# One copy and two stores at the end of a decode block, and a bias load in eight pieces

## The chip, the cores and the metric

The kernel runs on one core of one Trainium2 chip. The core has five engines that run side by side: TensorE for matrix products, VectorE, ScalarE and GpSimd for elementwise work, and SyncE, which issues DMAs and waits. DMAs are issued from SyncE's and from ScalarE's queue and carried out by 16 DMA engines. The metric is the device time of one execution in microseconds (us), as the median of several runs; the span of a profile is a little shorter than that time (188.2 us in a run that took 190.38).

## The reference

One decode step for a batch of two rows of 448 numbers. The normalised row goes into two branches, and both are added to the input. Branch A is attention over the last 4096 positions of a cache (16 query heads, 8 key heads of 256), branch B a dense pair with the Mish activation and a bias `b1`.

```python
x = A_x                                   # [2, 1, 448]
xn = layernorm(x)
q = (xn @ A_wq)                           # 16 heads of 256
p = softmax(q k^T / 16)                   # the last 4096 positions of the cache
A = (p v) @ A_wo                          # [2, 1, 448]
h = xn @ B_w1 + B_b1                      # [2, 1, 1792]
B = (h * tanh(softplus(h))) @ B_w2        # [2, 1, 448]
out = x + A + B
```

## The kernel before

The sum `x + A + B` is held in PSUM by TensorE. It is not kept as 2 rows of 448, but as four groups of 112 columns: group g stands on the partitions 32g and 32g+1 (one per batch row), so that four products can stand side by side in the array. The shape of the sum and its seed, and the way everything is added to it:

```python
x_bf = consts.tile([Bsz, D], BF16)                       # Bsz = 2, D = 448
nc.scalar.dma_start(out=x_bf[:, :], in_=A_x.flatten_outer_dims())      # L125
b1_sb = consts.tile([P, 2, NI], BF16)                    # P = 128, NI = 7
nc.scalar.dma_start(out=b1_sb[:], in_=B_b1.rearrange("(k q c) -> q k c", k=2, q=P))  # L127
load_k(0, 0)                                             # SyncE: keys, wq, keys, w1 ...
...
id2 = consts.tile([Bsz, Bsz], FP32)
nc.vector.tensor_copy(out=id2[:], in_=ident[0:Bsz, 0:Bsz])
...
nc.scalar.activation(out=rstd[:], in_=mv[:, 1:2], func=ACT.Sqrt, ...)  # L160, layernorm
nc.vector.reciprocal(out=rstd[:], in_=rstd[:])
... # VectorE: xn, masks, rows of xn; TensorE turns them; VectorE writes xs (L220)
early = ps_e.tile([Bsz, D], FP32)       # x and the first heads of A are summed here
acc = ps_a.tile([P, DG], FP32)          # DG = 112: the sum in four groups

def carry():                            # early -> acc, which starts the four groups
    e_sb = small.tile([P, 2 * Dh], FP32, tag="vs", name="e_sb", bufs=1)[0:Bsz, 0:D]
    nc.scalar.copy(out=e_sb, in_=early[:])
    for g in range(G):                  # G = 4
        nc.tensor.matmul(
            acc[32 * g : 32 * g + Bsz, :],
            lhsT=id2[:],
            rhs=e_sb[:, g * DG : (g + 1) * DG],
            start=True, stop=False, skip_group_check=True,
        )

def add_rows(lhsT, rows, stop=False):   # L249: the last heads of A, and all of B
    for g in range(G):
        nc.tensor.matmul(acc[32 * g : 32 * g + Bsz, :], lhsT=lhsT,
                         rhs=rows[:, g * DG : (g + 1) * DG], start=False, stop=stop, ...)
...
# VectorE turns each load of keys (L269); mish() reads b1_sb (L518)
```

The end of the program, behind the last part of the dense output:

```python
finish(u)
mix(u)
for part in range(len(w2_parts)):
    dense_out(part)                     # 56 products of L249, in parts as w2 lands

res = consts.tile([Bsz, D], BF16)
for g in range(G):
    dst = res[:, g * DG : (g + 1) * DG]
    src = acc[32 * g : 32 * g + Bsz, :]
    if g % 2 == 0:
        nc.vector.tensor_copy(out=dst, in_=src)          # L620
    else:
        nc.scalar.copy(out=dst, in_=src)                 # L622
nc.sync.dma_start(out=out.flatten_outer_dims(), in_=res[:])   # L623
```

Of the kernel before, what the change touches and what calls it, by code (L numbers as in the profile page):

```python
# [11 lines left out]
BF16 = mybir.dt.bfloat16  # L12
FP32 = mybir.dt.float32
# [4 lines left out]
def kernel(  # L18
# [13 lines left out]
    nc = tc.nc  # L32
    P = 128
    G = 4
# [4 lines left out]
    Bsz, Sq, D = A_x.shape  # L39
# [21 lines left out]
    DG = D // G  # L61
# [13 lines left out]
    consts = ctx.enter_context(tc.tile_pool(name="consts", bufs=1))  # L75
# [48 lines left out]
    x_bf = consts.tile([Bsz, D], BF16)  # L124
    nc.scalar.dma_start(out=x_bf[:, :], in_=A_x.flatten_outer_dims())  # L125
    b1_sb = consts.tile([P, 2, NI], BF16)
    nc.scalar.dma_start(out=b1_sb[:], in_=B_b1.rearrange("(k q c) -> q k c", k=2, q=P))  # L127

    load_k(0, 0)
    wq_t = []  # L130
# [7 lines left out]
    ident = consts.tile([P, P], BF16)  # L138
# [2 lines left out]
    nc.gpsimd.memset(qd[:], 0.0)  # L141
    ones = consts.tile([P, P], BF16)
    nc.gpsimd.memset(ones[:], 1.0)
    id2 = consts.tile([Bsz, Bsz], FP32)
    nc.vector.tensor_copy(out=id2[:], in_=ident[0:Bsz, 0:Bsz])
    hot = consts.tile([P, KU, 4, 32, KU], BF16)
    nc.gpsimd.memset(hot[:], 0.0)
    for k in range(KU):
        nc.gpsimd.tensor_copy(
            out=hot[:, k, :, :, k], in_=ident[:].rearrange("p (q y) -> p y q", y=4)  # L150
# [10 lines left out]
        out=rstd[:], in_=mv[:, 1:2], func=ACT.Sqrt, bias=eps_t[:], scale=1.0  # L161
# [4 lines left out]
        out=xn_bf[:],  # L166
# [8 lines left out]
        out=parm[:], in_=ident[:].rearrange("p (a o) -> p o a", o=2), axis=AXIS.X, op=ALU.add  # L175
# [3 lines left out]
        out=jm[:],  # L179
        in_=ident[:].rearrange("p (a j h) -> p j a h", j=J, h=rep),  # L180
# [4 lines left out]
        out=jm[:], in0=jm[:], scalar1=-1.0, scalar2=29952.0, op0=ALU.add, op1=ALU.mult  # L185
# [3 lines left out]
        out=mneg[:], in_=jm[:].unsqueeze(1).to_broadcast([P, TH * 8, J])  # L189
    )  # L190
    sel = consts.tile([P, 2, NQ], FP32)
    for x in range(2):
        for w in range(4):
            at = 32 * w + (2 * (w % 2) + x) * NQ
            src = ident[:, at : at + NQ]
            if w == 0:
                nc.vector.tensor_copy(out=sel[:, x, :], in_=src)
            else:
                nc.vector.tensor_tensor(
                    out=sel[:, x, :], in0=sel[:, x, :], in1=src, op=ALU.add  # L200
# [16 lines left out]
    for odd in range(2):  # L217
        for half in range(2):
            o = (half + odd) % 2
            nc.vector.tensor_scalar(  # L220
                out=xs[:, odd::2, half * Bsz : (half + 1) * Bsz],
# [10 lines left out]
    acc = ps_a.tile([P, DG], FP32)  # L232

    def carry():
        e_sb = small.tile([P, 2 * Dh], FP32, tag="vs", name="e_sb", bufs=1)[0:Bsz, 0:D]
        nc.scalar.copy(out=e_sb, in_=early[:])
        for g in range(G):
            nc.tensor.matmul(
                acc[32 * g : 32 * g + Bsz, :],
                lhsT=id2[:],  # L240
                rhs=e_sb[:, g * DG : (g + 1) * DG],
                start=True,
                stop=False,
                skip_group_check=True,
            )
# [31 lines left out]
    for n in range(2):  # L277
        for e in range(2):
# [3 lines left out]
                out=sp[:],  # L282
                in_=ident[:, o : o + 63 : 2].unsqueeze(1).to_broadcast([P, G, 32]),
# [316 lines left out]
    for g in range(G - 1):  # L600
        values(u, g)
        if g == 0:
            relay(u - 1)
            mix_early(u - 1)
            carry()
# [6 lines left out]
    for part in range(len(w2_parts)):  # L612
        dense_out(part)

    res = consts.tile([Bsz, D], BF16)
    for g in range(G):
        dst = res[:, g * DG : (g + 1) * DG]
        src = acc[32 * g : 32 * g + Bsz, :]
        if g % 2 == 0:
            nc.vector.tensor_copy(out=dst, in_=src)  # L620
        else:
            nc.scalar.copy(out=dst, in_=src)  # L622
    nc.sync.dma_start(out=out.flatten_outer_dims(), in_=res[:])  # L623


# [28 lines left out]
```

The softmax here doesn't subtract the row's maximum and nothing guards it: scores larger than these inputs give would overflow.

## Time and profile before

| what | value |
|---|---|
| time, median of 3 runs | 190.56 us (190.56 to 190.72) |
| span of the profile | 188.2 us |
| TensorE busy | 92.1 us (49%) |
| VectorE busy | 89.1 us (47%) |
| ScalarE busy | 12.3 us (7%) |
| moved by DMA | 77.78 MB, 413 GB/s on average |

The profile gives each engine's busy time, the span in 40 slices with a digit for the busy tenths of each, the DMA queues, the chain of waits that ended last (followed back from the last instruction), and the groups of instructions, each with its tile, its shape and what ended the idle time before it. In the lines, PE is TensorE's matmul, PEld its loading of weights, DVE VectorE, ACT ScalarE, SPq and ACTq the queues on which SyncE and ScalarE issue DMAs; q1 is SyncE's DMA queue, q10 ScalarE's. L620 is line 620 of the kernel. Names of tiles are without their numbers, so that `b_sb` is `b1_sb`, and `w<-in_B_w_dram` is a load of `w1` or `w2`.

### The profile page before, as it was taken

The page shows a single profiled execution, that of the slowest core. Times are in us where ns is not written, and L with a number is a line of the kernel's source. Part 1 is how long each engine was busy: PE and PEld are TensorE (multiplying, and loading weights), DVE is VectorE, ACT ScalarE, POOL GpSimd, SP SyncE. Part 2 cuts the span into 40 slices and gives each one's busy share as a digit, 9 for nine tenths or more (in the row PEclk, how much of TensorE's full clock was granted, in tenths as well). Part 3 has the DMA queues.
Part 4 walks back from the last instruction along what each step waited for, and adds up shares of the span by engine and source line. Part 5 has one row for each costly group of instructions (what it writes and reads, how often), then busy time and mean ns, then how long its engine had stood idle before and what let it go on. Part 6 is the DMA issues. An engine that isn't in the chain of part 4 may idle for free.

```text
span 188.2 us, 1989 instructions
## 1 busy us (share of the span) xinstructions
PE 92.1 (49%) x873; PEld 37.6 (20%) x873; DVE 89.1 (47%) x81; ACT 12.3 (7%) x23; POOL 4.0 (2%) x16
## 2 busy tenths in 40 slices
PE   0301545564139003888647033868464044968473
PEld 0100121521013001423112011413121011513261
DVE  6619643984980098008940395029910692040001
ACT  3000031001000100110001000110001001011101
POOL 8000000000000000000000000000000000000000
PEclk9999999558555855555556655555558555559965
DMA  6999999999999999999999999999998999999990
GB/s 223 446 390 409 440 432 428 470 442 390 428 449 418 428 426 411 466 446 400 435 463 411 414 435 434 429 442 414 463 460 383 418 431 432 435 398 452 411 391 31
DMA packets 5871, 77.78 MB, mean 413 GB/s; under 512 B 868, under 2 KB 1640, under 8 KB 2408
## 3 DMA queue, kind: packets, MB, share of 16 engines
q1 hardware_dynamic: 5588, 77.66, 96.8%
q8 instruction: 6, 0.10, 0.2%
q10 hardware_dynamic: 276, 0.01, 0.1%
q14 instruction: 1, 0.01, 0.0%
HBM read 77.67 MB, written 0.00 MB: 413 GB/s over the span
## 4 chain that ended last, share of the span: by engine, by line
DMA 80%; PE 10%; DVE 3%; issue 3%; SPq 2%; ACT 1%; DVEq 0%
DMA v<-in_A_v_cache_dram 59%; DMA k<-in_A_k_cache_dram 15%; DMA w<-in_B_w_dram 6%; PE pv L392 5%; DVE kt L269 2%; PE sc L347 2%; PE o L412 1%; PE acc L249 1%; PE dn L370 1%; SPq L134 1%; SPq L97 1%; DVE p L358 0%; SPq L105 0%; ACT ex L355 0%; ACT vs L406 0%
## 5 line engine op out<-in xcount | busy, mean ns | idle before, releaser
L269 DVE STREAM_TRANSPOSE kt<-k 128x4096 f32<-128x4096 f32 x16 | 70.0, 4414 | 39.9 <-DMA k<-in_A_k_cache_dram 39.9
L392 PE MATMUL pv<-v,p 128*32 128x512 bf16 x240 | 26.8, 593 | 54.1 <-DMA v<-in_A_v_cache_dram 54.1
L347 PE MATMUL sc<-kt,qd 128*32 128x512 bf16 x256 | 27.3, 599 | 3.2 <-DVE kt L269 1.9
L392 PEld LDWEIGHTS <-p 128*32 128x32 bf16 x240 | 8.4, 124 | 70.8 <-issue 65.2
L439 DVE TENSOR_TENSOR oT<-o,rec 128x16 bf16<-128x16 f32 x4 | 0.7, 174 | 28.8 <-PE o L412 16.3
L358 DVE STREAM_TRANSPOSE p<-ex 128x512 bf16<-128x512 bf16 x8 | 5.2, 690 | 16.0 <-ACT ex L355 16.0
L347 PEld LDWEIGHTS <-qd 128*32 128x32 bf16 x256 | 8.6, 134 | 19.8 <-issue 17.9
L355 ACT ACTIVATE ex<-sc 128x512 bf16<-128x512 f32 x8 | 4.8, 597 | 74.1 <-PE sc L347 74.1
L291 PE MATMUL q_ps<-wq,xs 128*32 128x512 bf16 x28 | 3.4, 624 | 11.8 <-DMA wq<-in_A_wq_dram 11.8
L474 PE MATMUL early<-wo,ox 128*2 128x448 bf16 x24 | 8.0, 500 | 0.8 <-ACT ox L464 0.8
L412 PE MATMUL o<-sel,vs 128*128 128x8 f32 x32 | 6.7, 339 | 2.8 <-ACT vs L406 2.8
L412 PEld LDWEIGHTS o<-sel,vs 128*128 128x128 f32 x32 | 6.4, 293 | 6.0 <-ACT vs L406 6.0
L370 PE MATMUL dn<-p,ones 128*128 128x512 bf16 x8 | 4.3, 541 | 6.0 <-DVE p L358 6.0
L406 ACT COPY vs<-pv 128x512 f32<-128x512 f32 x4 | 2.3, 586 | 49.4 <-PE pv L392 49.4
L504 PE MATMUL h_ps<-xs,w 128*128 128x4 bf16 x49 | 2.8, 193 | 4.6 <-DMA w<-in_B_w_dram 4.6
L336 PE MATMUL sc<-mneg,ident 128*128 128x512 bf16 x8 | 4.8, 594 | 0.0
L212 PE MATMUL xr_ps<-ident,xrows 2*128 2x2 bf16 x7 | 1.0, 181 | 6.6 <-DVE xrows L211 6.6
L378 DVE TENSOR_REDUCE rec<-dn 128x8 f32<-128x512 f32 x4 | 2.8, 692 | 2.5 <-PE dn L370 2.5
L291 PEld LDWEIGHTS <-xs 128*32 128x32 bf16 x28 | 1.0, 126 | 13.8 <-issue 13.8
L504 PEld LDWEIGHTS <-w 128*128 128x128 bf16 x49 | 2.7, 157 | 5.2 <-DMA w<-in_B_w_dram 5.2
L474 PEld LDWEIGHTS <-ox 128*2 128x2 bf16 x24 | 2.3, 105 | 4.6 <-issue 3.0
L455 PEld LDWEIGHTS <-hot 128*64 128x64 bf16 x48 | 2.0, 141 | 2.8 <-issue 2.8
(62 smaller groups left out, 37.7 us busy)
## 6 DMA issues: line engine op xcount, KB each, us to landing
k<-in_A_k_cache_dram SPq DMA_DIRECT2D x8, 4096.0 KB, 30.0
v<-in_A_v_cache_dram SPq DMA_DIRECT2D x15, 2048.0 KB, 27.0
wo<-in_A_wo_dram SPq DMA_DIRECT2D x3, 896.0 KB, 23.7
wq<-in_A_wq_dram SPq DMA_DIRECT2D x1, 2048.0 KB, 16.7
w<-in_B_w_dram SPq DMA_DIRECT2D x1, 1568.0 KB, 31.9
wq<-in_A_wq_dram SPq DMA_DIRECT2D x1, 1536.0 KB, 19.7
v<-in_A_v_cache_dram SPq DMA_DIRECT2D x1, 1536.0 KB, 9.7
wo<-in_A_wo_dram SPq DMA_DIRECT2D x2, 448.0 KB, 15.4
```

What stands on the lines that cost most here:

```text
L269: nc.vector.transpose(out=kt[i][:, :, :, r, :], in_=t[:, r * KE : (r + 1) * KE].bitcast(FP32).rearrange("p (a c j) -> p a c j", c=P // (R ...
L291: nc.tensor.matmul(q_ps[32 * u : 32 * (u + 1), :], lhsT=xs[:, s, :], rhs=wq_t[s][:, u * 512 : (u + 1) * 512], start=(s == 0), stop=(s == N ...
L336: nc.tensor.matmul(sc[:].rearrange("p t c m -> p (t c m)"), lhsT=ident[:], rhs=mneg[:].rearrange("p a j -> p (a j)"), start=True, stop=Fal ...
L347: nc.tensor.matmul(sc[32 * w : 32 * (w + 1)].rearrange("p t c m -> p t (c m)"), lhsT=qd[:, u, 2 * n + e, :, :].rearrange("p g q -> p (g q) ...
L355: nc.scalar.activation(out=ex[:, :, :, i, :], in_=sc[:], func=ACT.Exp, scale=scale)
L358: nc.vector.transpose(out=p_t[h][:].rearrange("p g t q -> p t g q"), in_=ex[:, h * TH : (h + 1) * TH].rearrange("p t c i m -> p t (c i m)" ...
L370: nc.tensor.matmul(dn[:].rearrange("p a q -> p (a q)"), lhsT=ones[:], rhs=p_t[i][:].rearrange("p g t q -> p (g t q)"), start=(i == 0), sto ...
L378: nc.vector.tensor_reduce(out=rec[:], in_=dn[:].rearrange("p a q -> p q a"), axis=AXIS.X, op=ALU.add)
L392: nc.tensor.matmul(pv[32 * w : 32 * (w + 1), :, :].rearrange("p x d -> p (x d)"), lhsT=p_t[a // 4][:, g, 4 * (a % 4) : 4 * (a % 4) + 4, :] ...
L412: nc.tensor.matmul(po[:, c, :], lhsT=sb[:, x, c::2], rhs=sel[:, x, :], start=(x == 0 and c == 0), stop=(last and x == 1), skip_group_check ...
L474: nc.tensor.matmul(early[:], lhsT=ox[:, i, :], rhs=w[:, i, :], start=False, stop=(u == U - 2 and i == 7),)
L504: nc.tensor.matmul(h_ps[:, i, :, :].rearrange("p k b -> p (k b)"), lhsT=w1_v[:, s, i, :], rhs=xs[:, s, 0 : 2 * Bsz], start=(s == 0), stop= ...
```

## The change

The last step is rearranged. The sum stands on the partitions 0, 1, 32, 33, 64, 65, 96 and 97. In place of four copies of two partitions, two on VectorE and two on ScalarE, one VectorE copy takes all 98 partitions from 0 to 97. The copied tile then holds the row of batch b in four runs of 112 numbers, on the partitions b, 32+b, 64+b and 96+b. Two stores bring them to their places in the output: ScalarE issues that of batch row 0, SyncE that of batch row 1.

So that the partitions in between hold something defined, the seed of the sum is widened: the identity is 2x32 in place of 2x2 (the other 30 columns are zero), and the seeding product writes all 32 partitions of each group. Apart from that, the diff cuts the load of the bias into eight loads of 16 partitions each, all on ScalarE's queue.

```diff
     b1_sb = consts.tile([P, 2, NI], BF16)
-    nc.scalar.dma_start(out=b1_sb[:], in_=B_b1.rearrange("(k q c) -> q k c", k=2, q=P))
+    b1_in = B_b1.rearrange("(k q c) -> q k c", k=2, q=P)
+    for lo in range(0, P, 16):
+        nc.scalar.dma_start(out=b1_sb[lo : lo + 16], in_=b1_in[lo : lo + 16])
@@
-    id2 = consts.tile([Bsz, Bsz], FP32)
-    nc.vector.tensor_copy(out=id2[:], in_=ident[0:Bsz, 0:Bsz])
+    id2 = consts.tile([Bsz, 32], FP32)
+    nc.vector.tensor_copy(out=id2[:], in_=ident[0:Bsz, 0:32])
@@ carry()
-                acc[32 * g : 32 * g + Bsz, :],
+                acc[32 * g : 32 * (g + 1), :],
                 lhsT=id2[:],
@@ the end
-    res = consts.tile([Bsz, D], BF16)
-    for g in range(G):
-        dst = res[:, g * DG : (g + 1) * DG]
-        src = acc[32 * g : 32 * g + Bsz, :]
-        if g % 2 == 0:
-            nc.vector.tensor_copy(out=dst, in_=src)
-        else:
-            nc.scalar.copy(out=dst, in_=src)
-    nc.sync.dma_start(out=out.flatten_outer_dims(), in_=res[:])
+    last = 32 * (G - 1) + Bsz
+    res = consts.tile([P, DG], BF16)
+    nc.vector.tensor_copy(out=res[0:last, :], in_=acc[0:last, :])
+    rows = out.rearrange("b s (g e) -> b (s g) e", g=G)
+    for b, queue in ((0, nc.scalar), (1, nc.sync)):
+        queue.dma_start(out=rows[b], in_=res[b : last - 1 + b : 32, :])
```

## The prediction

> **What bounds the kernel now.** I read the page's slices first, because they tell whether one resource is full from end to end. Each digit is the busy share of a slice of 4.7 us, in tenths:
>
> ```profile
> DMA  6999999999999999999999999999998999999990
> GB/s 223 446 390 409 440 432 428 470 442 390 428 449 418 428 426 411 466 446 400 435 463 411 414 435 434 429 442 414 463 460 383 418 431 432 435 398 452 411 391 31
> q1 hardware_dynamic: 5588, 77.66, 96.8%
> q10 hardware_dynamic: 276, 0.01, 0.1%
> ```
>
> The 16 DMA engines are busy in all but the first and the last slice, and 96.8% of what they can do is spent on SyncE's queue (q1), which carries 77.66 MB. So the kernel is a stream of loads with a short head and a short tail. ScalarE's queue (q10) costs 0.1%. The chain of waits says the same from the other side: 80% of the span is DMA, and from 2.52 us on the chain goes from one load to the next. Then I read its last pieces (start, length, what):
>
> ```profile
> 172.06 12.12 DMA w<-in_B_w_dram
> 184.17 0.04 issue
> 184.22 0.78 PE acc L249 x17
> 184.99 0.20 issue
> 185.19 0.45 PE acc L249 x11
> 185.64 0.24 DVE res L620
> 185.89 0.30 DVEq L649
> ```
>
> The last load lands at 184.17 us and the span ends at 188.2, so 4.0 us stand behind the stream. They belong to 28 matmuls (to 185.64), the copies of the sum, the store and the end of the program. The timeline gives the copies and the store, and the waits of SyncE give the landing of the store:
>
> ```profile
> 185.62 0.56 DVE L620 CAST res<-acc 2x112 bf16<-2x112 f32 x2 [3.63 <-PE acc L249]
> 185.66 0.52 ACT L622 CAST res<-acc 2x112 bf16<-2x112 f32 x2 [7.60 <-PE acc L249]
> 186.25 0.33 SPq L623 DMA_DIRECT2D out_dram<-res  x1
> SPq L649 <- DMA out_dram<-res: 0.6, 1, 0.6
> ```
>
> Two copies run one behind the other on each engine, so both are done at 186.18 us, and the store is issued 0.07 us later. The issue ends at 186.58, SyncE then waits 0.6 us for the data to land, about 187.2, and the last 1.0 us is the closing of the program. Last, the diff splits the bias load, so I looked at the head of the timeline:
>
> ```profile
> 0.73 0.53 ACTq L125 DMA_DIRECT2D x_bf<-in_A_x_dram  x1
> 1.29 0.42 ACTq L127 DMA_DIRECT2D b_sb<-in_B_b_dram  x1
> 1.75 1.28 ACT L160 ACT_TABLE_LOAD   x1 [1.75 <-issue]
> 3.08 0.29 ACT L160 ACTIVATE rstd<-mv,eps_t 2x1 f32<-2x1 f32 x1
> 7.75 0.61 DVE L220 TENSOR_SCALAR xs<-xr_ps,parm 128x8 bf16<-128x8 bf16 x4 [0.35 <-PE xr_ps L212]
> 13.22 8.77 DVE L269 STREAM_TRANSPOSE kt<-k 128x4096 f32<-128x4096 f32 x2 [4.86 <-DMA k<-in_A_k_cache_dram]
> 40.31 0.19 DVE L518 TENSOR_TENSOR h_sb<-h_ps,b_sb 128x28 f32<-128x28 f32 x1
> ```
>
> The reader should see that ScalarE loads its table and computes rstd only after its DMA issues, that VectorE's early work ends at 8.36 us (7.75 plus 0.61) and then stands idle for 4.86 us until the first keys land, and that the bias is not read before 40.31 us although it lands 17.0 us after its issue.
>
> **What the Trainium skill says.** The page "VectorE: DVE Perf Modes", section on the TRN2 errata, gives 120 cycles plus one per element of the free dimension for a VectorE copy out of PSUM, at 0.96 GHz, and 172 plus one per element for ScalarE, at 1.2 GHz. For 112 elements that is an estimate of 242 ns and 237 ns. The trace has 266 and 245 ns, so it agrees within a tenth, and no term of the formula depends on the number of partitions. The page "DMA: Bandwidth & Descriptors", section "Issuing engines are not separate DMA queues", says that issuing from several engines saves only the time of issue. Here that is 0.33 us at most, and there is only one store to begin with. The same page, section "Why a DMA increments its semaphore by 16 and not by 1", says that a DMA is spread over as many engines as divide its slowest dimension, up to 16, each adding one semaphore write. The count of q10 fits exactly: x is 2 runs and 2 writes, the bias 256 runs (128 partitions by 2) and 16 writes, 276 in all. The same page's "Specifications" name 512 B as the smallest transfer at full rate, with a read-modify-write below. The old store has two rows of 896 B, the new runs are 224 B. No run here shows what that costs for a store.
>
> **The change part by part.**
>
> 1. The copies. Four copies go and one comes. It has the same 112 elements per partition, so I take 0.27 us from the row of L620. It must wait for the last group of the sum, where the first old copy waited for group 0 alone. The last 11 matmuls take 0.45 us, one of them 0.25 to 0.30, so they follow each other at (0.45 - 0.27)/10 = 0.018 us, and three of them are 0.05 us. New copy: from 185.62 + 0.05 = 185.67 to 185.94. Old end 186.18, so -0.24 us.
>
> 2. The stores. One store on SyncE becomes one on SyncE and one on ScalarE, both released by that copy. SyncE's issue moves forward with it: 0.24 earlier and again 0.33 long. ScalarE's issues in this trace took 0.53 and 0.42 us, but both were at the very start, beside SyncE's, where a load of keys took 0.65 against 0.54 later on. Taking 0.12 off, ScalarE's store lies between 0.33 and 0.42, and I charge +0.05 for it being the later of the two. If it is as slow as the two at the start, it is +0.09 to +0.20.
>
> 3. Landing. 1.8 KB in 8 runs in place of 2 moves nothing in bandwidth. For short runs and the second landing I put +0.03; this is a guess in size, bounded by the 0.6 us of the old wait.
>
> 4. The bias in eight loads. ScalarE issues eight in place of one: 1.29 + 8 x (0.42 + 0.04) = 5.0 us, in place of 1.75. The table load and rstd move by 3.2 us, and with them everything VectorE does in order behind rstd: xs is done at 8.36 + 3.2 = 11.6 us. The keys land for VectorE at 13.22, so 1.6 us of the idle 4.86 remain. Nothing reaches the chain. In the DMA engines 8 x 16 semaphore writes replace 16, so 112 small packets more. q10 took 0.1% of 16 engines for 276 packets, 0.19 us per engine; 112 more are 0.19 x 112/276 = 0.08 us per engine, an upper estimate, as a semaphore write carries less than a run. As the DMA engines are the bound, I count +0.05.
>
> 5. The wider identity (2x32) and the carry that writes 32 rows per group. The carry sits at 173.28, eight passes within 0.37 us, and at 176.33 TensorE has waited 1.71 us for the next values. 112 columns stream through either way, and the cast of the identity runs in VectorE's early part. 0.00.
>
> Sum: -0.24 + 0.05 + 0.03 + 0.05 = -0.11 us. 190.56 - 0.11 = 190.45; I say 190.43, as the upper estimate of part 4 is likelier too high than too low.
>
> **The rivals.**
>
> The first: the tail gives nothing, because the new wait takes the place of the old. ScalarE's issue of 0.53 us and a slower landing of short runs eat the 0.24. For it: 0.53 stands in the head of the trace. Against it: that is the first DMA of the program. It makes 190.6 to 190.8.
>
> The second: VectorE's head becomes late. If an issue on ScalarE cost 0.7 us, with SyncE issuing its own loads up to 3.90 us, rstd would be late by 1.29 + 8 x 0.7 - 1.75 = 5.1 us, over the 4.86 of slack, and the first transposition with it, by 0.3 us. Against its mattering: a transposition sets when the next load of keys is issued (22.02 us), and at that time loads issued before 3.90 us are still landing until 35 us, so the DMA engines would not run dry. It makes 190.4 to 190.7.
>
> The third: the bias load helps. One load of 256 runs on q10 alternates with large packets, 17.0 us to land; in eight loads the pieces might disturb the stream less, or more. In slices 2 to 4, where it lands, the stream moves (446 + 390 + 409)/3 = 415 GB/s, where the windows of 20 us between 40 and 160 us have 430 on average; 3.5% of 14 us is 0.5 us that might be won or doubled. Against it: slices 10, 19 and 31 are as low with no bias in flight. It makes 190.0 or 191.0.
>
> A fourth, that the tail is hidden, can be struck out: nothing runs beside it.
>
> **Range and chances.** The three runs of before lie within 0.16 us. The tail may move the time by -0.24 to +0.1, the stream by up to 0.3 either way. I put the range from 190.05 to 190.80. The 2% mark is 3.8 us: the whole tail behind the last load is 4.0 us and the part the change touches is under 1 us, so faster by 2% is out of reach, and slower would need the stream itself to be disturbed in a way no view hints at. Faster 0.01, same 0.98, slower 0.01.
>
> **What would show it.** One copy of 98x112 at 0.25 to 0.29 us that ends about 0.30 us behind the last matmul, where the old copies ended 0.54 us behind it (186.18 less 185.64). Two stores issued within 0.1 us of each other, ScalarE's below 0.45 us. q10 with 276 + 112 + 4 + 4 = 396 packets and q1 with 5588 - 4 + 8 = 5592. xs done near 11.6 us, and the first transposition of keys still released by the DMA near 13.2. The last load of the dense weights landing within 0.3 us of 184.17. I am wrong if that landing moves by more, if ScalarE's store lands later than the old one did, or if the first transposition is released by VectorE's own work instead of by the keys.

## The result and the profile after

The changed kernel takes 191.35 us, where the kernel before took 190.57 beside it: a ratio of 1.0036, with a 95% interval of 1.0023 to 1.0049. That is slower by 0.7 us (0.4 to 0.9). The prediction was 190.43 us, with a range of 190.05 to 190.80. It had the change within 2%, and the sign of the small difference wrong.

The slices of the changed kernel's page show that the stream of loads is what it was. Each digit is the busy tenth of a slice, and the two last lines are the queues of SyncE and ScalarE with packets, MB and share:

```profile
DMA  6989999999999999999999999989999999999980
GB/s 222 444 381 417 450 416 429 465 440 388 443 478 423 395 417 453 416 436 433 423 464 436 395 440 468 443 378 430 430 436 440 419 418 444 430 411 433 408 344 7
q1 hardware_dynamic: 5592, 77.66, 96.3%
q10 hardware_dynamic: 396, 0.01, 0.1%
```

The packets are the 5592 and 396 that were worked out from runs and semaphore writes. The tail, from the last 11 products of the sum on, from the timeline of the changed kernel (start, length, engine and line, work):

```profile
185.57 0.45 PE L251 MATMUL acc<-w,act_bf 128*2 128x112 bf16 x11 [0.30 <-issue]
186.07 0.27 DVE L619 CAST res<-acc 98x112 bf16<-98x112 f32 x1 [3.82 <-PE acc L251]
186.37 0.67 SPq L622 DMA_DIRECT2D out_dram<-res  x1
186.37 0.58 ACTq L622 DMA_DIRECT2D out_dram<-res  x1
```

And from the waits of SyncE's queue, what it waited for in us, how often, and the longest:

```profile
SPq L648 <- DMA out_dram<-res: 1.1, 2, 0.7
```

The copy does what it was meant to do. It takes 0.27 us, and 0.30 us after its start the stores are issued, where the four copies took 0.63 (from 185.62 to 186.25). It starts 0.07 us later behind the products, as it waits for all four groups, so counted from the start of the last 11 products to the store's issue, 186.25 - 185.19 = 1.06 us became 186.37 - 185.57 = 0.80: a gain of 0.26. But each of the two issues takes about twice the 0.33 us of the one store before, and the landing is waited for 1.1 us in place of 0.6. From the store's issue to the end of the span there were 188.2 - 186.25 = 1.95 us, and now there are 189.2 - 186.37 = 2.83 (spans are given to 0.1 us; unrounded, the trace has 2.00 and 2.84).

The head has changed as well, and further than predicted. From the timeline of the changed kernel, in three windows:

```profile
1.32 12.35 ACTq L129 DMA_DIRECT2D b_sb<-in_B_b_dram  x8
7.22 4.03 SPq L136 DMA_DIRECT2D wq<-in_A_wq_dram  x2
...
13.71 1.28 ACT L162 ACT_TABLE_LOAD   x1 [13.71 <-DMA k<-in_A_k_cache_dram]
15.00 0.29 ACT L162 ACTIVATE rstd<-mv,eps_t 2x1 f32<-2x1 f32 x1
...
20.14 8.76 DVE L271 STREAM_TRANSPOSE kt<-k 128x4096 f32<-128x4096 f32 x2
```

ScalarE is held in its eight issues until 13.7 us, by a landing of keys. rstd comes 12 us later than before, SyncE's second load 5.8 us later (7.22 for 1.44), and VectorE's first transposition 6.9 us later (20.14 for 13.22), now without waiting for its keys. The old issue of SyncE's second load, from the timeline of the kernel before:

```profile
1.44 1.04 SPq L134 DMA_DIRECT2D wq<-in_A_wq_dram  x2
```

Two suspects therefore stood side by side: the two stores and the eight bias loads.

### The profile page after: what moved, and what is told of

It is laid out like the page before. It is cut to its first block, busy times and chain, and to the rows that moved or that the text cites. A ratio compares the mean times of both kernels' runs of the same rounds, so it can differ in the third digit from the quotient of the medians.

```text
span 189.2 us, 1995 instructions
## 1 busy us (share of the span) xinstructions
PE 91.1 (48%) x870; PEld 38.0 (20%) x873; DVE 88.6 (47%) x80; ACT 11.8 (6%) x21; POOL 3.9 (2%) x16
## 3 DMA queue, kind: packets, MB, share of 16 engines
q1 hardware_dynamic: 5592, 77.66, 96.3%
## 4 chain that ended last, share of the span: by engine, by line
DMA 80%; PE 9%; DVE 3%; issue 3%; SPq 1%; ACTq 1%; ACT 1%; DVEq 0%
DMA v<-in_A_v_cache_dram 58%; DMA k<-in_A_k_cache_dram 10%; DMA w<-in_B_w_dram 6%; DMA b_sb<-in_B_b_dram 6%; PE pv L394 5%; DVE kt L271 2%; PE sc L349 2%; PE o L414 1%; PE acc L251 1%; PE dn L372 1%; SPq L105 1%; ACTq L129 0%; DVE p L360 0%; ACT ex L357 0%; ACT vs L408 0%
## 5 line engine op out<-in xcount | busy, mean ns | idle before, releaser
L349 PE MATMUL sc<-kt,qd 128*32 128x512 bf16 x256 | 28.0, 611 | 4.6 <-DVE kt L271 2.3
L214 PEld LDWEIGHTS <-xrows 2*128 2x128 bf16 x7 | 0.7, 99 | 18.7 <-DVE xrows L213 18.5
L338 PE MATMUL sc<-mneg,ident 128*128 128x512 bf16 x5 | 3.0, 591 | 0.0
## 6 DMA issues: line engine op xcount, KB each, us to landing
w<-in_B_w_dram SPq DMA_DIRECT2D x1, 1568.0 KB, 20.2
```

What stands on the lines that cost most here:

```text
L338: nc.tensor.matmul(sc[:].rearrange("p t c m -> p (t c m)"), lhsT=ident[:], rhs=mneg[:].rearrange("p a j -> p (a j)"), start=True, stop=Fal ...
L349: nc.tensor.matmul(sc[32 * w : 32 * (w + 1)].rearrange("p t c m -> p t (c m)"), lhsT=qd[:, u, 2 * n + e, :, :].rearrange("p g q -> p (g q) ...
```

## The experiments

Ratios are to the kernel before, run beside each on the same chip (its medians there were 190.71 to 190.81 us), with 95% intervals. "Stretch" is the time from the first issue of a store to the end of the span, good to 0.05 us.

**Which of the two it is.** First, the changed kernel with its bias load whole:

```diff
-    for lo in range(0, P, 16):
-        nc.scalar.dma_start(out=b1_sb[lo : lo + 16], in_=b1_in[lo : lo + 16])
+    nc.scalar.dma_start(out=b1_sb[:], in_=b1_in)
```

> The changed kernel with its bias load put back into one DMA. Theory: two things slow the changed kernel. Eight bias loads use up the eight completion semaphores of the DMAs, so that SyncE's loads and ScalarE's eighth piece wait (SyncE's second load is issued at 7.22 us in place of 1.44, rstd comes at 15.00 in place of 3.08), which costs the stream 0.2 to 0.4 us at its end; and the two stores cost 0.6 to 0.9 us where one copy saves 0.24. Then this kernel is at 191.0 (190.9 to 191.15), its last dense weights land within 0.1 us of 184.17, and the stretch from the first store's issue to the end of the span stays at 2.8 us. Rival: the bias split is harmless and the whole loss is in the tail: 191.3 to 191.4.

It took 191.56 us, ratio 1.0036 (1.0024 to 1.0048), as much above before as with eight loads. The theory (0.4 us above the 190.57 of before) fell, and the rival (0.7 to 0.8 above) held: 0.7 again, beside a kernel before that was at 190.81 here. From its timeline:

```profile
186.32 0.66 SPq L620 DMA_DIRECT2D out_dram<-res  x1
```

ScalarE's issue takes 0.58 us here. The stretch is 189.3 - 186.32 = 2.98 us. The loss is in the tail.

Second, the reverse: the kernel before with only its bias load cut into eight.

> The kernel before with only its bias load cut into eight. Theory: the semaphores run out, rstd comes at about 15 us, and the stream ends 0.2 to 0.4 us later: 190.8 to 190.95, with the tail from the store's issue to the end unchanged at 1.95 us. Rival: harmless, 190.5 to 190.65.

190.93 us, ratio 1.0009 (1.0001 to 1.0018): 0.17 us (0.02 to 0.34), just clear of nothing, and between the two sides (0.2 to 0.4 us and at most 0.1). Its stretch is 2.0 us, so the split does not reach the tail; the head is held up as in the changed kernel (rstd at 15.06 us). A delay of 12 us at the head costs at most 0.34 us.

**What in the stores.** Third, the kernel before with one store per whole row, on two queues:

```diff
-    nc.sync.dma_start(out=out.flatten_outer_dims(), in_=res[:])
+    rows = out.flatten_outer_dims()
+    for b, queue in ((0, nc.scalar), (1, nc.sync)):
+        queue.dma_start(out=rows[b : b + 1], in_=res[b : b + 1, :])
```

> The kernel before with its four copies and its one bias load, and only the store divided: batch row 0 from ScalarE's queue, batch row 1 from SyncE's, each a whole row of 896 B in place of four runs of 224 B. Theory: two stores side by side are what costs, whatever their runs: both issues take 0.55 to 0.7 us in place of 0.33 and the last landing is waited for 1 us in place of 0.6; 191.2 to 191.4. Rival: the short runs cost, and two stores of whole rows cost only the longer issue: 190.75 to 190.95.

190.87 us, ratio 1.0007 (0.9999 to 1.0015). Both issues are short, although side by side. From its timeline:

```profile
186.58 0.31 SPq L625 DMA_DIRECT2D out_dram<-res  x1
186.59 0.25 ACTq L625 DMA_DIRECT2D out_dram<-res  x1
```

Two stores on two queues do not cost 0.7 us by themselves: the theory of this run had fallen, and so had the longer issue that its rival gave them.

Fourth, the changed kernel with its bias load whole and both stores on SyncE:

```diff
-    for b, queue in ((0, nc.scalar), (1, nc.sync)):
+    for b, queue in ((0, nc.sync), (1, nc.sync)):
```

> The changed kernel with its bias load whole and both stores issued by SyncE, one behind the other. Theory: two issues side by side share what makes the descriptors, so one behind the other is no slower: two issues of 0.33 us, the second done 0.66 to 0.72 us after the copy, and the same time as with the bias load whole and two queues within 0.1 us (about 191.0). Rival: the second queue itself costs[...]: 0.2 us or more faster than with two queues, 190.6 to 190.8.

191.85 us, ratio 1.0051 (1.0039 to 1.0063), the slowest of the tails. Its timeline has both issues in one line:

```profile
186.28 1.28 SPq L620 DMA_DIRECT2D out_dram<-res  x2
```

With no neighbour on another queue an issue still takes about 1.28/2 = 0.64 us. So it is not a collision that makes it long but the store itself: something in its shape. Both expectations missed: an issue of these stores is not 0.33 us long, and the second queue is not what costs. The Trainium skill says in "DMA: Bandwidth & Descriptors", "Issuing engines are not separate DMA queues", that issuing from several engines saves only the issuing time. Here two queues save 1.28 - 0.66 = 0.62 us of it, but the stretch, 189.5 - 186.28 = 3.22 us, is only 0.24 us longer than with two queues, and the time 0.29 us: with one queue the landing is waited for 0.9 us in place of 1.2.

**What in the shape.** A store of the change differs from the old one in two ways: its runs are 224 B in place of 896, and it reads every 32nd partition in place of neighbours. Three runs take these apart, together with a second profile of the kernel before.

> The kernel before once more, unchanged, for a second profile. In five profiles with the same loads behind 170 us, the last matmuls of the sum began between 185.19 and 185.57 us, and the kernel before had the earliest. If that scatter is the stream's own, this profile begins them anywhere from 185.2 to 185.6 and its stretch from the store's issue to the end is again 1.95 us (within 0.1). If the changes moved the stream, it is at 185.19 again, within 0.1.

190.61 us. The last matmuls began at 185.34 and the stretch is 188.4 - 186.40 = 2.00 us:

```profile
186.40 0.33 SPq L623 DMA_DIRECT2D out_dram<-res  x1
```

The kernel before differs from itself by 0.15 us at the end of its stream. In the other profiles with the same loads the last matmuls began between 185.41 and 185.90 us; why is not shown, and no edit is held responsible for it. The readings below use the stretch, which begins behind it.

The changed kernel with its bias load whole, its stores reading neighbours. What it stores is not the sum: only the first of the eight partitions read hold it, the others come from the seed.

```diff
-        queue.dma_start(out=rows[b], in_=res[b : last - 1 + b : 32, :])
+        queue.dma_start(out=rows[b], in_=res[4 * b : 4 * (b + 1), :])
```

> The changed kernel with its bias load whole, one copy and two stores of four runs, but the stores read the neighbouring partitions 0 to 3 and 4 to 7 in place of every 32nd; what they store is not the sum, and the work is the same. Theory (the step of 32 partitions costs): both issues fall from 0.66 and 0.58 us to 0.25 to 0.40 and the wait for the landing from 1.2 to 0.7, so that the copy's gain shows: 0.5 to 0.8 us faster than with the step, that is 0.3 us below to 0.1 above the kernel before. Rival (short runs or four partitions cost): as slow as with the step, 0.6 to 0.8 us above before.

190.76 us, ratio 1.0006 (0.9997 to 1.0014), against 1.0036 with the step. The timeline:

```profile
186.39 0.28 DVE L617 CAST res<-acc 98x112 bf16<-98x112 f32 x1 [4.09 <-PE acc L249]
186.69 0.34 SPq L620 DMA_DIRECT2D out_dram<-res  x1
186.70 0.28 ACTq L620 DMA_DIRECT2D out_dram<-res  x1
```

The same copy, the same runs of 224 B, the same two queues, and the issues are down at 0.34 and 0.28 us. The stretch is 189.0 - 186.69 = 2.31 us. The step was worth 2.98 - 2.31 = 0.67 us of it, and by the ratios 0.30% or 0.57 us. What is left over the old 2.00, 0.3 us, stands behind the issue. It eats the 0.26 us that the copy gains.

The other way round, from the kernel before: two long rows, one plain store, but the second row read from partition 32. That row holds zeros, so the second row of the output is left out.

```diff
-    res = consts.tile([Bsz, D], BF16)
+    res = wide                      # 64 x 448, cleared at the start
...
-    nc.sync.dma_start(out=out.flatten_outer_dims(), in_=res[:])
+    nc.sync.dma_start(out=out.flatten_outer_dims(), in_=res[0:33:32, :])
```

> The kernel before with its four copies and one store of two whole rows of 896 B, but the store takes its second row from partition 32 (a row of zeros) in place of partition 1; the second output row is left out so. Theory (the step of 32 partitions costs): the issue takes 0.55 to 0.7 us in place of 0.33, and the stretch from the issue to the end grows from 1.95 to 2.2 to 2.6 us: slower than before by 0.3 to 0.6 us. Rival (short runs cost): no change, within 0.1 us.

191.20 us, ratio 1.0025 (1.0015 to 1.0036). The store has the 2 runs of 896 B that it had before, on one queue:

```profile
186.55 0.64 SPq L625 DMA_DIRECT2D out_dram<-wide  x1
```

The step alone doubles the issue, from 0.33 to 0.64 us, and lengthens the stretch to 189.0 - 186.55 = 2.45 us.

Then short runs without a step: the kernel before with a padded tile, so that each row is four runs of 224 B on one partition.

```diff
-    res = consts.tile([Bsz, D], BF16)
+    res = consts.tile([Bsz, G, P], BF16)
...
-    nc.sync.dma_start(out=out.flatten_outer_dims(), in_=res[:])
+    nc.sync.dma_start(out=out.rearrange("b s (g e) -> (b s) g e", g=G), in_=res[:, :, 0:DG])
```

> The kernel before with its one store, but the tile it stores from is padded, so that each batch row is four runs of 112 numbers (224 B) on one partition in place of one run of 896 B; the two partitions are still neighbours. Theory: it is the step of 32 partitions that makes the issue slow (0.62 us in place of 0.33) and the landing late, so short runs on neighbouring partitions change nothing: 190.6 to 190.9 beside the same before, the issue at 0.33 to 0.40 us, the stretch from the issue to the end at 2.0 us. Rival: the short runs do it: the issue at 0.55 us or more, or the landing 0.4 us later; slower than before by 0.4 to 0.8 us.

191.46 us, ratio 1.0041 (1.0029 to 1.0054), and the slowest single issue of all:

```profile
186.60 0.82 SPq L623 DMA_DIRECT2D out_dram<-res  x1
```

Here my theory, that only a step of partitions makes an issue slow, fell in its "only". The program lists this store as 8 by 1 by 112. It is no longer a plain block of neighbouring rows either, and it pays for it. Short runs as such are not what costs at the issue: the neighbouring-partition stores have the same 224 B and 0.28 to 0.34 us.

Behind the issue, the traces show when the data move. Each line is the first 2 us from the first issue, in 40 slices of 0.05 us, of the kernel before, the two stores of neighbouring partitions, the one store of two whole rows with a step, and the two stores of four partitions with a step (bias load whole):

```profile
GB/s 0 0 0 0 0 0 0 0 0 0 0 0 0 0 18 18 0 0 0 0 0 0 0 0 0 0 0 0 0 0 0 0 0 0 0 0 0 0 0 0
GB/s 0 0 0 0 0 0 0 0 0 0 0 0 0 0 0 5 27 5 0 0 0 0 0 0 0 0 0 0 0 0 0 0 0 0 0 0 0 0 0 0
GB/s 0 0 0 0 0 0 0 0 0 0 0 0 0 0 0 0 0 0 0 0 0 0 0 0 18 18 0 0 0 0 0 0 0 0 0 0 0 0 0 0
GB/s 0 0 0 0 0 0 0 0 0 0 0 0 0 0 0 0 0 0 0 0 0 0 0 0 9 9 0 0 0 0 0 9 5 5 0 0 0 0 0 0
```

The data of one store move within 0.1 us in every case, as short runs or long. What differs is when they set out: with the step about half a microsecond later, of which 0.3 us is the longer issue. And two stores with a step, issued at the same time from two queues, set out one behind the other, 0.37 us apart; two without a step go together. The record of landings in the same traces divides the stretch (unrounded, us; the last landing counts):

| stores | issue | end of issue to landing | landing to end of span |
|---|---|---|---|
| one, two whole rows (before, both profiles) | 0.33 | 0.83 | 0.83 to 0.84 |
| two, a whole row each | 0.31 | 0.98 | 0.83 |
| two, neighbouring partitions | 0.34 | 1.01 | 0.94 |
| one, two whole rows with a step | 0.64 | 1.00 | 0.84 |
| one, four runs per row | 0.82 | 1.01 | 0.83 |
| two with a step (bias load whole) | 0.66 | 1.33 | 0.94 |
| two with a step (the change) | 0.67 | 1.34 | 0.83 |

The last column is not the stores' doing: it is 0.90 and 0.96 in the two other profiles with the old tail and a divided bias load. A second store costs 0.15 us in the landing even as whole rows, and short runs on neighbouring partitions add next to nothing to that (0.98 to 1.01). The writing of short runs into the output is thus not what makes the change slow.

**Any step, or the reach over the partitions?** The same two stores, reading every second partition; again not the sum:

```diff
-        queue.dma_start(out=rows[b], in_=res[b : last - 1 + b : 32, :])
+        queue.dma_start(out=rows[b], in_=res[b : b + 7 : 2, :])
```

> The changed kernel with its bias load whole, its one copy and its two stores, which read every second partition (0, 2, 4, 6 and 1, 3, 5, 7) in place of every 32nd; what they store is not the sum. If any step other than one makes the issue slow: both issues at 0.55 to 0.7 us, 0.5 to 0.8 us above before. If it is the reach over four quarters of the 128 partitions: issues at 0.25 to 0.40 us and at most 0.25 us above before, as with neighbouring partitions.

191.37 us, ratio 1.0034 (1.0021 to 1.0048). From its timeline:

```profile
186.47 0.76 SPq L620 DMA_DIRECT2D out_dram<-res  x1
186.47 0.67 ACTq L620 DMA_DIRECT2D out_dram<-res  x1
```

A step of two is no better than 32, so it is not the reach over the partitions.

**Can the one copy be kept?** Four stores of two neighbours each, two on each queue, write the same output as the change:

```diff
-    for b, queue in ((0, nc.scalar), (1, nc.sync)):
-        queue.dma_start(out=rows[b], in_=res[b : last - 1 + b : 32, :])
+    for g in range(G):
+        queue = nc.scalar if g % 2 == 0 else nc.sync
+        queue.dma_start(out=rows[:, g * DG : (g + 1) * DG], in_=res[32 * g : 32 * g + Bsz, :])
```

> The changed kernel with its bias load whole and its one copy, but four stores of two neighbouring partitions each (one per group, 2 x 112 numbers), two on each queue, in place of two stores of every 32nd partition; the output is the reference's. If the step is what costs, each issue takes 0.28 to 0.36 us, two behind one another 0.6 to 0.7, and the end is as with the two stepped stores or 0.3 us better: 0.3 to 0.7 us above before. If short runs or the stepped rows of the output cost as well, each issue takes 0.5 us or more: 1.0 us above before or worse.

191.17 us, ratio 1.0020 (1.0013 to 1.0027). Two issues behind one another take 0.63 us on SyncE and 0.57 on ScalarE, as long as one stepped store, and the landing is waited for 1.0 us. Its ratio is below the 1.0036 of the stepped stores, and still above before.

**A shorter end by fewer copies.** From the kernel before, the sum in two groups of 224 columns:

```diff
-    acc = ps_a.tile([P, DG], FP32)
+    acc = ps_a.tile([P, DA], FP32)         # DA = 224, two groups
...                                         # carry, add_rows and the copies: 2 groups of 224
```

> A try at a faster end, from the kernel before: the sum stands in two groups of 224 columns in place of four of 112, so that one copy on VectorE and one on ScalarE, side by side, do the whole and the store stays one plain store of two rows. By the copies of 112 columns at 0.27 and 0.25 us and one element per cycle, a copy of 224 takes 0.35 to 0.40 us in place of the 0.56 of two: -0.18. Only two products stand side by side in the array: the last 11 or 12 products become 6 and take 0.1 to 0.3 us longer. Sum -0.1 to +0.15: 190.6 to 190.9 beside a before of 190.7.

191.25 us, ratio 1.0029 (1.0018 to 1.0039), over the expected range. The copies came out as worked out (0.38 us on VectorE, 0.34 on ScalarE), the products did not:

```profile
183.41 2.82 PE L251 MATMUL acc<-w,act_bf 128*2 128x224 bf16 x28
186.27 0.38 DVE L622 CAST res<-acc 2x224 bf16<-2x224 f32 x1 [4.36 <-PE acc L251]
```

The products run for 2.82 us without a wait for the weights: in this profile TensorE has become the bound behind the last loads, and the copies start at 186.27 in place of 185.62 to 185.98 in the profiles with four copies and one bias load. The profile is of one of the fastest of 21 executions (190.70 us, where they reach 191.85), so what makes the median 0.55 us slower than before is shown only in part.

**Why ScalarE was held.** The program lists what each DMA waits for. There are eight completion semaphores for all DMAs of the two issuing engines, given out in turn, and a DMA that gets a semaphore for the second time waits until its first holder has landed. In the kernel before, seven DMAs start at the head. In the changed one, the eighth bias load gets the semaphore of the first key load, which explains the 13.36 us at which it is issued. If that is so, seven pieces give the same semaphore to SyncE's second load, and the stream itself must stop:

```diff
-    nc.scalar.dma_start(out=b1_sb[:], in_=B_b1.rearrange("(k q c) -> q k c", k=2, q=P))
+    b1_in = B_b1.rearrange("(k q c) -> q k c", k=2, q=P)
+    for lo, hi in ((0, 16), (16, 32), (32, 48), (48, 64), (64, 80), (80, 96), (96, P)):
+        nc.scalar.dma_start(out=b1_sb[lo:hi], in_=b1_in[lo:hi])
```

> The kernel before with its bias load in seven pieces (six of 16 partitions and one of 32). Theory of the eight semaphores: now the seventh piece waits for the load of x, long landed, and SyncE's second load has to wait for the semaphore of its first, the 4 MB of keys. So rstd comes early again (at 5 to 7 us in place of 15), but the DMA engines run dry once those keys have landed at 10.5 to 13.5 us, for 1.5 to 2.5 us: 192.0 to 193.3, slower than with eight pieces by over 1 us. Rival (the small runs of the bias disturb the stream, or ScalarE's issues are slow by themselves): about as with eight pieces, 190.7 to 191.0.

193.84 us, ratio 1.0161 (1.0146 to 1.0176), slower by 3.1 us: one piece fewer than eight, and dearer by 2.9. It is over the expected range (193.3 at most); the stop is as foretold and a little longer. The slices and the head of the timeline:

```profile
DMA  6959999999999999998999999999999999999990
GB/s 219 424 233 328 427 448 438 444 434 397 431 482 441 386 420 413 495 438 379 431 458 431 397 434 461 431 407 424 448 434 424 431 434 420 431 407 441 413 374 19
```

```profile
13.93 0.86 SPq L136 DMA_DIRECT2D wq<-in_A_wq_dram  x2
```

SyncE's second load is issued at 13.93 us in place of 1.44, and the third slice is half empty: 233 and then 328 GB/s, where before had 390 and 409. rstd comes at 6.25 us, since ScalarE is free again. So the semaphores are shown, and so is why eight pieces are nearly harmless: there SyncE's loads waited only for small pieces, and its second was issued at 7.22 us, while the first keys were still landing.

## Why the prediction was wrong

**What bounds the kernel** was right: a stream of loads, a tail that nothing covers, and a change that works in that tail.

**Part 1, the copies,** was right: -0.24 us was counted, with the later start of the one copy, and from the last 11 products to the store's issue 1.06 us became 0.80, a gain of 0.26.

**Part 2, the stores, is the step that failed first.** It said that SyncE's issue "moves forward" and is "again 0.33 long", and put +0.05 for ScalarE's. The length was taken over from a store of another shape. Measured: 0.67 us on SyncE and 0.58 on ScalarE, so +0.34. The prediction looked for the danger in the second queue, and at the issue there is none; two whole-row stores are issued in 0.31 and 0.25 us side by side. What takes the time is the step between partitions: two rows with a step take 0.64, four neighbours 0.34.

**Part 3, the landing,** failed by more: +0.03 was put, as a guess, and from the end of the issue to the last landing 0.83 us became 1.34, so +0.51. The experiments divide it: a second store costs 0.15 us even with whole rows, short runs add 0.03, and the step the remaining 0.3 (1.01 to 1.33), as the later of the two stores then sets out behind the other. Each of these sizes is from single profiles, and why the two go one behind the other is open. The bound that the guess leaned on was misread as well: the 0.6 us of waiting is not the whole way to the landing, since SyncE begins that wait 0.28 us after its issue ends. The old landing was at 187.41 us and not at about 187.2, and the closing of the program takes 0.83 us and not 1.0.

**Part 4, the bias,** had the size nearly right by a wrong way. Counted was +0.05 us; alone it is 0.17 (0.02 to 0.34), and together with the stores it doesn't show (1.0036 with and without). That is luck, for it foresaw ScalarE free at 5.0 us and xs at 11.6. It was 13.7 and 20.2, because the step counted only time of issue and no wait for a semaphore. The slack of VectorE that it relied on was overrun by 7 us, which is one of the signs of being wrong that the prediction named; another, a later landing of ScalarE's store, came true as well (188.00 us in place of 187.41). What saved the time is that the DMA engines did not run dry: slices 2 to 4 have 444, 381 and 417 GB/s, and before had 446, 390 and 409. The second rival had concluded so, from loads issued before 3.90 us; all but the first were issued later, from 7.22 us on, the next two while the first keys were still landing. Where the 0.17 us arises is open.

**Part 5** is right as far as it shows: the cast of the identity took 1.03 us where it took 1.48, one seeding product 0.27 us where it took 0.25, and neither is anywhere near the tail.

**The rivals.** The first, that "the new wait takes the place of the old", is the one that came true, by a cause that it didn't name, and by 0.5 us more than its 190.6 to 190.8. The sum in the predicted terms: copies -0.26, issue +0.34, landing +0.51, bias 0 to +0.2. That is +0.6 to +0.8, and 0.7 was measured.

## What to carry to other kernels

At an uncovered end, count a store by its shape and not by its bytes: in these runs one plain block of neighbouring partitions was issued in 0.3 us, and the same bytes with a step between partitions, or as several runs per partition, in 0.6 to 0.8 us, and they then set out later too. Count up to the landing, and not only the waiting that the issuing engine shows. An instruction saved on a compute engine can be lost to that. A load cut into pieces takes as many completion semaphores as pieces: list what the DMAs of the program wait for before cutting, since one piece more or less may decide whether a small transfer or the main stream is held.

## What the runs showed that was not expected

- A step of 2 partitions is as slow to issue as one of 32 (0.76 and 0.67 us against 0.66 and 0.58).
- 1792 B in two rows on two neighbouring partitions cost 0.82 us to issue when each row was cut into four runs, and 0.33 us as whole rows.
- Two stores with a step, issued at the same time from two queues, moved their data 0.37 us apart; two stores of neighbouring partitions moved theirs together.
- One bias piece fewer made the kernel 2.9 us slower, because the order in which eight semaphores come round put the wait on the other engine.
- The norm's result can be 12 us late, and the first transposition 7 us, at a cost of 0.2 us.
